# Two units' logits in one run of TensorE, on seven buffers for squares, in a fused Fourier, MLP and soft-MoE kernel

## The chip, the cores and the metric

One of the eight cores of a Trainium2 chip runs the whole program. The metric is the device time of one execution in microseconds. The kernel before took 2180.7 us as the median of three runs (2176.5 to 2181.17).

## What is computed

The reference runs three stages on `x` (8 sequences of 3072 tokens of 256 numbers):

```python
Y = irfft(soft_shrink(rfft(x, axis=1) @ (w_r + i w_i) + b))      # 24576 tokens x 256
h = np.maximum(Y @ w_in, 0.0);  z = (h * h) @ w_out              # MLP, 2048 hidden
logits = z @ phi                                                 # 32 slots
d = softmax(logits, over all tokens);  slot_in = d.T @ z         # 32 x 256
slot_out[e] = relu(slot_in[e] @ w1[e]) @ w2[e]                   # 8 experts, 4 slots each
out = softmax(logits, over slots) @ slot_out
```

The change lies in the second and third line of it: the MLP's hidden squares, their logits, and the sum over tokens that the dispatch softmax weighs. `phi` is multiplied into `w_out` ahead of time (`pw`), so logits come straight from the squares.

## The kernel before

A first part (about 530 us) does the Fourier transforms and leaves the tokens in DRAM. Then a loop does the MLP, the logits and the running dispatch sum; a tail of some 100 us does the experts and writes the output. The change is in the loop, and the order in which the loop's Python statements stand is the order of each engine's queue: the schedule is written out by hand, and an engine takes its instructions in that order.

The loop goes over 32 superblocks (`sb`) of 768 tokens, and in each over 8 units, so that n = 8 sb + r runs from 0 to 257, with r from 0 to 7. A `Unit` is 256 hidden columns for the superblock's tokens, in four quarters of 128 x 384 (`part(0)` to `part(3)`). Its work is spread over three iterations. In iteration n, `cur` is unit n, `p1` is unit n-1, `p2` is unit n-2:

- Products (TensorE, three matmuls each, `product`): `p0`, `p1`, `p5` of `cur`; `p4`, `p6`, `p2`, `p3` of the unit before. They go to the banks psA, psX (two of each, by parity of the unit) and psZ. `p0` and `p5` are each followed by a copy of psA to psX on ScalarE (L708, L716), onto which the next product of psX accumulates.
- The iteration's order on TensorE is p0, p4, p6, p1, p5, p2, p3, then `logits` of `p2` (tile `ls`). `add(3)` on VectorE (L735) reads psX after `p6`; `p3` accumulates onto the same psX and so waits for it. `add(1)` reads psA after `p2`.
- `relu` (ScalarE, L739) and `square` (L743) on GpSimd, but for `square(0)`, mostly on VectorE. `turn(1)` and `turn(0)` (VectorE, L747) transpose the squares into `gt` for the dispatch sum.
- `logits` multiplies the four quarters by `pw` with four matmuls on four 32-column strips, two records each.

Beside this, one superblock later, the routing of the block before (`s = sb - 1`) goes on at fixed r: `apart` at the end of r1 (ScalarE copies half of the logits, L807), `scores`, `lowest`, `exponents` and `weights` at r2 (maximum, exponentials, transposed through DRAM into `ee` by SP's queue, L828 and L830), the softmax over slots and `into_slots` at r3: 192 matmuls of 32 x 32 (`pz`, L765) into four banks. The iteration r4 has an order of its own (`else`): there `collect` (VectorE, L770) adds the four banks to `acc` while the next products start.

`stage_d` prepares the tokens of the superblock to come: at r0 and r1 two fills of 64 small matmuls (psY, L459), ScalarE's copies of them, and then some 20 casts and subtractions on GpSimd, of which `step(r, k)` lets k go at iteration r. `load_z` (SP) loads the tile `zt` for the one after that at the end of r5.

The squares lie in five buffers: three that the first halves take in turn, two for the second halves (`self.g`). The routing's scratch (`lw`, `lv`, `ew`, `et`, `co`) lies beside them in the same tile `wg`.

Of the kernel before, what the change touches and what calls it, by code (L numbers as in the profile page):

```python
# [29 lines left out]
TOK = TB * N1  # L30
# [73 lines left out]
def fft_moe_kernel(ctx, tc, x, w_r, w_i, b_r, b_i, moe_w_in, moe_w_out, moe2_phi, moe2_w1, moe2_w2,  # L104
# [384 lines left out]
    with tc.manual_schedule():  # L489
# [185 lines left out]
        def flat(o, n):  # L675
            return wgf[:, o:o + n]

        OG, OL, OZ, OE, OS = 0, 5 * GR, 5 * GR + TOK, 5 * GR + 3 * TOK, 6 * GR + 3 * TOK

        class Unit:  # L680


            def __init__(self, m):
                self.m = m
                self.s, i = divmod(m, NW)
                self.q = QS[self.s % 2][i]
                self.first, self.last = i == 0, i == NW - 1
                self.n = f"{self.s}_{self.q}"
                self.g = [flat(OG + GR * (m % 3), GR), flat(OG + GR * (3 + m % 2), GR)]

# [99 lines left out]

        lw, lv = flat(OL, HT), flat(OL + HT, HT)
        ew, et, co = (flat(OE + HT * i, HT) for i in range(3))
        ee = flat(OS, GR)
# [8 lines left out]

        def apart():

            for h in range(2):
                w, v = (slice(64 * i, 64 * i + 64) for i in (h, 1 - h))
                nc.scalar.copy(lv[w], lgp[v, HT * h:HT * h + HT])  # L807

        def scores():
            for h in range(2):  # L810
                w = slice(64 * h, 64 * h + 64)
                nc.vector.tensor_tensor(out=lw[w], in0=lgp[w, HT * h:HT * h + HT], in1=lv[w], op=ALU.add)

        def lowest(s):
            nc.vector.tensor_reduce(out=bx, in_=lw, axis=AX.X, op=ALU.max)
            nc.vector.scalar_tensor_tensor(out=nm[(s + 1) % 3], in0=bx, scalar=-1.0, in1=nm[s % 3], op0=ALU.mult, op1=ALU.min)

        def exponents(s):
            no, nn = nm[s % 3], nm[(s + 1) % 3]
            al[s], se[s] = (rt.tile([128, 1], F32, tag=t, name=f"{t}{s}", bufs=2) for t in ("al", "se"))  # L820
            nc.scalar.activation(out=ew, in_=lw, func=AF.Exp, bias=nn, accum_out=se[s])
            nc.scalar.activation(out=al[s], in_=no, func=AF.Exp, bias=nn, scale=-1.0)

        def weights(s):

            nc.vector.transpose(et, ew)
            d = dram.tile([32, GR], F32, tag="ed", name=f"ed{s}", bufs=2)
            nc.sync.dma_start(out=d.rearrange("p (c n) -> c p n", c=4), in_=et)  # L828
            for a in range(4):
                nc.sync.dma_start(wgf[32 * a:32 * a + 32, OS:OS + GR], d)  # L830

        def turn_rows():
            nc.vector.transpose(lts, lw)
            return lts.rearrange("p (k n) -> p k n", n=32)
# [54 lines left out]
        NM = NSB * NW  # L889
        run = side = None  # L890
        for n in range(NM + 2):
# [11 lines left out]
            def route(at):  # L903
                return s is not None and r == at

            if run is None:
                if cur:
                    cur.p0()
                step(1, 1)
                if p1:  # L910
                    p1.p4()
                step(1, 1)
                if route(2):
                    scores()
                    lowest(s)
                    exponents(s)
                step(2, 2)
                if p2 and r != 2:
                    p2.turn(1)
                if p1:  # L920
                    p1.p6()
                    p1.add(3, p1.x)
                if route(2):
                    weights(s)
                if p2 and r == 2:
                    p2.turn(1)
                if cur:
                    cur.p1()
                    cur.p5()
                if p2 and r not in (2, 3):  # L930
                    p2.turn(0)
                if p1:
                    p1.p2()
                    p1.add(1, p1.a)
                if p2 and r in (2, 3):
                    p2.turn(0)
                step(1, 1)
                if p1:
                    p1.relu(3)
                    p1.square(3, nc.gpsimd)  # L940
                    p1.p3()
                    p1.square(2, nc.vector if n == NM else nc.gpsimd)
                    p1.relu(1)
                    p1.square(1, nc.vector if n == NM else nc.gpsimd)
                if cur:
                    cur.square(0, nc.vector)
                if route(3):
                    cur.p4()
                    cur.p6()
                    drain(over_slots(turn_rows()))  # L950
                    keep(s, co)
                if p2:
                    p2.logits()
            else:
                sr, ps = run
                run = None
                p2.logits()
                p1.p3()
                p1.square(3, nc.gpsimd)
                p1.square(2, nc.gpsimd)  # L960
                collect(sr, 0, ps[0])
                collect(sr, 1, ps[1])
                cur.p0()
                p1.p2()
                p1.add(1, p1.a)
                collect(sr, 2, ps[2])
                p1.relu(1)
                p1.square(1, nc.gpsimd)
                collect(sr, 3, ps[3])
                cur.p1()  # L970
                cur.p5()
                cur.square(0, nc.gpsimd)
                p2.turn(1)
                p2.turn(0)
# [4 lines left out]
            if route(1):  # L979
                apart()  # L980
            if route(3):
                total(s)
            if r == 0 and sb + 1 < NSB:
                side = stage_d(sb + 1, bank, nc.gpsimd)
                next(side)
            step(2, 3)
            step(3, 10)
# [5 lines left out]
            if route(3):  # L993
                ps = [bank_a(n + 1, f"pz{s}_a"), bank_x(n + 1, f"pz{s}_x")] + [bank(f"pz{s}_{i}") for i in range(2)]
                into_slots(s, ps)
                cur.add(3, cur.x)
                cur.relu(3)
                run = (s, ps)
            if sb == NSB - 1 and r == 0:
                t = zp.tile([128, TB, DM], F32, tag="zt", name="ez").rearrange("p t d -> p (t d)")  # L1000
                for k in range(2):
                    load_w1(t[:, FE * k:FE * k + FE])
                load_wo()

# [7 lines left out]

        warm(1, "warm0")
        apart()
        for k in range(3):
            load_w1(wg[:, k])
        scores()
        lowest(s)
# [4 lines left out]
        for c in range(4):  # L1023
            w = slice(32 * c, 32 * c + 32)
            nc.tensor.matmul(pe[c], lhsT=same[w], rhs=ew[w], start=True, stop=True)
        p = bank("p_m")
# [15 lines left out]
        into_slots(s, ps)  # L1042
        lt = turn_rows()
        for k in range(3, 6):
# [176 lines left out]
```

## Time and profile before

| | before |
|---|---|
| median of three runs | 2180.7 us |
| profiled execution | 2177.24 us, span 2175.0 us |
| mean granted TensorE clock | 0.977 |
| TensorE busy | 2080.6 us (96%) |
| VectorE busy | 1543.0 us (71%) |
| ScalarE busy | 1277.2 us (59%) |
| GpSimd busy | 1317.5 us (61%) |
| matmuls of `ls` | 2048 records, busy 219.6 us |

The profile is of one execution. Busy time is the union of an engine's instructions; a matmul's record is longer than its share of the array, since products overlap (a record of 0.33 us, the next one 0.17 us later). So what an operation costs on TensorE is read from the starts of successive records. Where a row names a releaser, the engine sat idle for the time in brackets until that instruction ended.

### The profile page before, as it was taken

The page shows a single profiled execution, that of the slowest core. Times are in us where ns is not written, and L with a number is a line of the kernel's source. Part 1 is how long each engine was busy: PE and PEld are TensorE (multiplying, and loading weights), DVE is VectorE, ACT ScalarE, POOL GpSimd, SP SyncE. Part 2 cuts the span into 40 slices and gives each one's busy share as a digit, 9 for nine tenths or more (in the row PEclk, how much of TensorE's full clock was granted, in tenths as well). Part 3 has the DMA queues.
Part 4 walks back from the last instruction along what each step waited for, and adds up shares of the span by engine and source line. Part 5 has one row for each costly group of instructions (what it writes and reads, how often), then busy time and mean ns, then how long its engine had stood idle before and what let it go on. Part 6 is the DMA issues. An engine that isn't in the chain of part 4 may idle for free.

```text
span 2175.0 us, 55408 instructions
## 1 busy us (share of the span) xinstructions
PE 2080.6 (96%) x22294; PEld 1598.3 (73%) x22294; DVE 1543.0 (71%) x2590; ACT 1277.2 (59%) x2910; POOL 1317.5 (61%) x1583
## 2 busy tenths in 40 slices
PE   8999999998899999999999999999999999999994
PEld 3888888887777777777777777777777777777743
DVE  2677677766577777777777777777777777777743
ACT  2667666754565566566556665655666666556632
POOL 0243344411777777777777777777777777777500
PEclk7999999998999999999999999999999999999995
DMA  8988898863011111111111111111111111111589
GB/s 245 263 242 238 232 231 235 237 152 94 16 36 27 29 36 32 27 27 32 31 29 30 39 27 27 29 34 29 27 41 27 27 27 36 29 27 46 169 302 396
DMA packets 113772, 210.02 MB, mean 97 GB/s; under 512 B 14092, under 2 KB 80908, under 8 KB 107244
## 3 DMA queue, kind: packets, MB, share of 16 engines
q1 hardware_dynamic: 112348, 203.31, 34.6%
q8 instruction: 175, 2.87, 0.6%
q10 hardware_dynamic: 1168, 3.18, 0.4%
q14 instruction: 81, 0.66, 0.1%
HBM read 122.64 MB, written 83.79 MB: 95 GB/s over the span
## 4 chain that ended last, share of the span: by engine, by line
PE 69%; DVE 13%; DMA 5%; ACT 4%; POOL 4%; issue 4%; SPq 1%; DVEq 0%; ACTq 0%; POOLq 0%
PE psX L701 14%; PE psA L701 12%; PE ls L754 7%; DVE gt L747 4%; PE psZ L701 4%; PE pz_a L765 4%; PE psB L247 4%; PE psC L331 4%; PE psY L459 3%; PE pz_x L765 3%; POOL wg L743 3%; PE pz L765 3%; DVE wg L735 3%; PE psA L214 2%; ACT wg L739 2%
## 5 line engine op out<-in xcount | busy, mean ns | idle before, releaser
L743 POOL TENSOR_TENSOR wg<-wg 128x384 f32<-128x384 f32 x797 | 707.3, 910 | 371.3 <-ACT wg L739 368.9
L747 DVE STREAM_TRANSPOSE gt<-wg 128x768 f32<-128x768 f32 x512 | 487.9, 962 | 172.2 <-POOL wg L743 171.9
L739 ACT ACTIVATE wg<-psX 128x384 f32<-128x384 f32 x512 | 251.8, 492 | 269.4 <-PE psX L701 217.6
L701 PE MATMUL psX<-yh,wia 128*128 128x384 f32 x1024 | 364.9, 356 | 39.1 <-DVE wg L735 36.1
L701 PE MATMUL psA<-yh,wia 128*128 128x384 f32 x1024 | 362.2, 359 | 0.0
L739 ACT ACTIVATE wg<-wg 128x384 f32<-128x384 f32 x512 | 267.8, 523 | 139.7 <-DVE wg L735 139.6
L701 PEld LDWEIGHTS psA<-yh,wia 128*128 128x128 f32 x1024 | 192.3, 188 | 103.4 <-DVE wg L735 42.6
L701 PEld LDWEIGHTS psX<-yh,wia 128*128 128x128 f32 x1024 | 192.5, 188 | 95.8 <-DVE wg L735 56.6
L123 POOL TENSOR_TENSOR Sl<-Sf,Sh 128x256 fp32r<-128x256 f32 x96 | 75.4, 786 | 274.2 <-ACT Sh L122 239.8
L754 PE MATMUL ls<-wg 128*32 128x384 f32 x2048 | 219.6, 499 | 0.3 <-DVE wg L743 0.3
L765 PE MATMUL pz_x<-gt,wg 32*32 32x512 f32 x1584 | 209.2, 597 | 0.0
L765 PE MATMUL pz_a<-gt,wg 32*32 32x512 f32 x1584 | 208.9, 596 | 0.0
L765 PE MATMUL pz<-gt,wg 32*32 32x512 f32 x2976 | 203.5, 597 | 0.0
L743 DVE TENSOR_TENSOR wg<-wg 128x384 f32<-128x384 f32 x227 | 195.8, 863 | 7.8 <-ACT wg L739 7.7
L708 ACT COPY psX<-psA 128x384 f32<-128x384 f32 x256 | 119.6, 467 | 120.1 <-PE psA L701 119.7
L701 PE MATMUL psA<-yl,wia 128*128 128x384 f32 x512 | 172.4, 337 | 0.0
L701 PE MATMUL psZ<-yh,wib 128*128 128x384 f32 x512 | 172.1, 336 | 0.0
L701 PE MATMUL psX<-yl,wia 128*128 128x384 f32 x512 | 172.0, 336 | 0.0
L701 PE MATMUL psX<-yh,wib 128*128 128x384 f32 x512 | 171.6, 335 | 0.0
L701 PE MATMUL psA<-yh,wib 128*128 128x384 f32 x512 | 171.5, 335 | 0.0
L735 DVE TENSOR_TENSOR wg<-psX,wg 128x384 f32<-128x384 f32 x256 | 137.1, 536 | 42.5 <-ACT wg L722 32.0
L735 DVE TENSOR_TENSOR wg<-psA,wg 128x384 f32<-128x384 f32 x256 | 136.1, 532 | 41.0 <-PE psA L701 39.0
(211 smaller groups left out, 4807.5 us busy)
## 6 DMA issues: line engine op xcount, KB each, us to landing
bt<-ad SPq DMA_DIRECT2D x96, 256.0 KB
zd<-sc SPq DMA_DIRECT2D x96, 256.0 KB
zt<-zd SPq DMA_DIRECT2D x64, 384.0 KB
xt<-in_x_dram SPq DMA_DIRECT2D x126, 192.0 KB
ad<-sa SPq DMA_DIRECT2D x112, 192.0 KB
out_dram<-ob SPq DMA_DIRECT2D x21, 1024.0 KB
wg<-ed SPq DMA_DIRECT2D x124, 96.0 KB
w<-in_moe_w_dram SPq DMA_DIRECT2D x5, 1024.0 KB
```

The costliest lines, as they stand in the source:

```text
L123: (eng or nc.vector).tensor_tensor(out=lo, in0=v, in1=f(hi), op=ALU.subtract)
L247: nc.tensor.matmul(p[:, dh, :, l], lhsT=t[:, l, 128 * dh:128 * dh + 128], rhs=bm[:, 2 * (u % NU) + l], start=True, stop=True)
L331: nc.tensor.matmul(ps[l][:, v], lhsT=cm[w, (u - 1 + v) % NU, c], rhs=ub[v][w, c], start=c == 0, stop=c == 1)
L459: nc.tensor.matmul(ps[g][64 * c:64 * c + 64, tt::TB], lhsT=zt[s][w, tt, d:d + 64], rhs=dmt[w], start=True, stop=True)
L701: nc.tensor.matmul(p, lhsT=w[:, k, l], rhs=r[:, j], start=start and n == 0, stop=n == 2, skip_group_check=True)
L708: nc.scalar.copy(self.x, self.a)
L735: nc.vector.tensor_tensor(out=self.part(k), in0=p, in1=self.z, op=ALU.add)
L739: nc.scalar.activation(out=t, in_=t if p is None else p, func=AF.Relu)
L743: eng.tensor_tensor(out=t, in0=t, in1=t, op=ALU.mult)
L747: nc.vector.transpose(gt[:, 2 * self.q + a + window(self.s)], self.g[a])
L754: nc.tensor.matmul(lgp[o:o + 32], lhsT=pw[:, 2 * self.q + a], rhs=self.part(k), start=self.first, stop=self.last, skip_group_check=True)
L765: nc.tensor.matmul(ps[a][32 * c:32 * c + 32], lhsT=ee[w, c, k], rhs=gt[w, o:o + NT2, 32 * j:32 * j + 32], start=k == 0, stop=k == NB6 - 1, ...
```

## The change

- `logits` is no longer issued once in every iteration for unit n-2. It is issued in odd iterations, but for r3, for units n-3 and n-2 one behind the other, and at the head of the iteration r4 for the units of r0 and r1. So in a superblock there are four runs of two units: at the end of r1, at the head of r4, at the end of r5 and of r7.
- Since squares live longer, there are seven buffers for them, four and three. The routing's scratch moves out of `wg` into the unused end of the tile `zt` that `stage_d` works on (for the last block it stays in `wg`). The last superblock's two loads of expert weights into the `zt` tile move from r0 to r5.
- At r2, `relu(3)` moves ahead of `weights` and of the other relus, and the two steps of `stage_d` that stood in mid-iteration (ScalarE's copies of the second fill) move to the iteration's end.
- At r3, `add(3)` and `relu(3)` of the unit of r3 no longer stand behind `into_slots`; they stand in r4 behind collects 0 and 1. In r4, `p0` comes ahead of `p3`, and `collect` 3 moves to the end of r5.

```diff
-        OG, OL, OZ, OE, OS = 0, 5 * GR, 5 * GR + TOK, 5 * GR + 3 * TOK, 6 * GR + 3 * TOK
+        OZ, OS = 7 * GR, 7 * GR + TOK
...
-                self.g = [flat(OG + GR * (m % 3), GR), flat(OG + GR * (3 + m % 2), GR)]
+                self.g = [flat(GR * (m % 4), GR), flat(GR * (4 + m % 3), GR)]
...
-        lw, lv = flat(OL, HT), flat(OL + HT, HT)
-        ew, et, co = (flat(OE + HT * i, HT) for i in range(3))
+        def scratch(s):
+
+            if s == NSB - 1:
+                z, o = wgf, 4 * GR
+            else:
+                z, o = zt[min(s + 2, NSB - 1)].rearrange("p t d -> p (t d)"), 2 * TOK
+            return [z[:, o + HT * i:o + HT * i + HT] for i in range(5)]
+
...
                 if route(2):
-                    scores()
+                    scores(s)
                     lowest(s)
                     exponents(s)
-                step(2, 2)
                 if p2 and r != 2:
                     p2.turn(1)
                 if p1:
                     p1.p6()
                     p1.add(3, p1.x)
+                if p1 and r == 2:
+                    p1.relu(3)
                 if route(2):
                     weights(s)
...
                 if p1:
-                    p1.relu(3)
+                    if r != 2:
+                        p1.relu(3)
                     p1.square(3, nc.gpsimd)
...
                 if route(3):
                     cur.p4()
                     cur.p6()
-                    drain(over_slots(turn_rows()))
-                    keep(s, co)
-                if p2:
+                    drain(over_slots(turn_rows(s)))
+                    keep(s, scratch(s)[4])
+                if n % 2 and p2 and not route(3):
+                    units[n - 3].logits()
                     p2.logits()
             else:
-                sr, ps = run
+                sr, ps = late = run
                 run = None
-                p2.logits()
+                units[n - 4].logits()
+                units[n - 3].logits()
+                collect(sr, 0, ps[0])
+                collect(sr, 1, ps[1])
+                p1.add(3, p1.x)
+                p1.relu(3)
+                cur.p0()
                 p1.p3()
                 p1.square(3, nc.gpsimd)
                 p1.square(2, nc.gpsimd)
-                collect(sr, 0, ps[0])
-                collect(sr, 1, ps[1])
-                cur.p0()
                 p1.p2()
+                collect(sr, 2, ps[2])
                 p1.add(1, p1.a)
-                collect(sr, 2, ps[2])
                 p1.relu(1)
                 p1.square(1, nc.gpsimd)
-                collect(sr, 3, ps[3])
                 cur.p1()
                 cur.p5()
...
-            step(2, 3)
+            if late and r == 5:
+                collect(late[0], 3, late[1][3])
+            step(2, 5)
             step(3, 10)
...
                 into_slots(s, ps)
-                cur.add(3, cur.x)
-                cur.relu(3)
                 run = (s, ps)
-            if sb == NSB - 1 and r == 0:
+            if sb == NSB - 1 and r == 5:
                 t = zp.tile([128, TB, DM], F32, tag="zt", name="ez").rearrange("p t d -> p (t d)")
                 for k in range(2):
                     load_w1(t[:, FE * k:FE * k + FE])
+            if sb == NSB - 1 and r == 0:
                 load_wo()
```

## Rows read from the trace of the kernel before

**Rows 1.** Busy us of each engine in a stretch, then clock, DMA share, GB/s
```profile
core 0: us, PE busy (x) PEld busy (x) DVE busy (x) ACT busy (x) POOL busy (x), PEclk, DMA share, GB/s
1000.00:1200.00 200.00, 195.39 (x2262) 148.77 (x2260) 152.80 (x240) 120.60 (x278) 153.48 (x183) 1.00 0.16 33
```

**Rows 2.** TensorE's waits over the span: total us, times, longest us
```profile
PE psX L701 <- DVE wg L735: 36.1, 63, 6.0
```

**Rows 3.** Timeline of TensorE, r6: start us, duration us; first, third of p0
```profile
1004.36 0.44 PE L701 MATMUL psA<-yh,wia 128*128 128x384 f32 x1
...
1004.82 0.34 PE L701 MATMUL psA<-yh,wia 128*128 128x384 f32 x1
...
1007.94 0.34 PE L701 MATMUL psX<-yh,wia 128*128 128x384 f32 x1
1008.21 0.85 PE L754 MATMUL ls<-wg 128*32 128x384 f32 x8
1008.99 0.45 PE L701 MATMUL psA<-yh,wia 128*128 128x384 f32 x1
1009.27 0.34 PE L701 MATMUL psA<-yl,wia 128*128 128x384 f32 x1
```

**Rows 4.** Timeline of TensorE, 1008.8 to 1008.9: the second four of that visit
```profile
1008.55 0.51 PE L754 MATMUL ls<-wg 128*32 128x384 f32 x4
```

**Rows 5.** Timeline of TensorE around the second psY fill, r1
```profile
1022.43 0.34 PE L701 MATMUL psA<-yh,wia 128*128 128x384 f32 x1
1022.70 1.15 PE L459 MATMUL psY<-dmt,zt 48*64 48x48 f32 x64
1023.78 0.45 PE L701 MATMUL psX<-yh,wia 128*128 128x384 f32 x1
```

**Rows 6.** Timeline of TensorE, r3: p1's first two, p2's last, p3's first
```profile
1031.64 0.44 PE L701 MATMUL psX<-yh,wia 128*128 128x384 f32 x1
1031.92 0.34 PE L701 MATMUL psX<-yl,wia 128*128 128x384 f32 x1
...
1033.14 0.34 PE L701 MATMUL psA<-yh,wia 128*128 128x384 f32 x1
1033.92 0.44 PE L701 MATMUL psX<-yh,wia 128*128 128x384 f32 x1 [0.44 <-DVE wg L735]
```

**Rows 7.** Timeline of TensorE, r4: p2's last and p1's first product
```profile
1045.27 0.34 PE L701 MATMUL psA<-yh,wia 128*128 128x384 f32 x1
1045.68 0.44 PE L701 MATMUL psX<-yh,wia 128*128 128x384 f32 x1
```

**Rows 8.** Timeline of TensorE, r5: p2's last and p3's first product
```profile
1049.78 0.34 PE L701 MATMUL psA<-yh,wia 128*128 128x384 f32 x1
1050.62 0.44 PE L701 MATMUL psX<-yh,wia 128*128 128x384 f32 x1 [0.51 <-DVE wg L735]
```

**Rows 9.** Timeline of ScalarE, r2 and r3: the fill's copies, r3's copy to psX
```profile
1028.25 0.83 ACT L476 COPY zt<-psY 128x384 f32<-128x384 f32 x2
...
1031.10 0.49 ACT L708 COPY psX<-psA 128x384 f32<-128x384 f32 x1
```

**Rows 10.** Timelines of VectorE and GpSimd, r6 to r7
```profile
1008.26 0.55 DVE L743 TENSOR_TENSOR wg<-wg 128x384 f32<-128x384 f32 x1
1008.31 1.19 POOL L743 TENSOR_TENSOR wg<-wg 128x384 f32<-128x384 f32 x1 [0.61 <-ACT wg L739]
...
1011.22 0.52 DVE L735 TENSOR_TENSOR wg<-psX,wg 128x384 f32<-128x384 f32 x1
```

**Rows 11.** Timelines of VectorE and GpSimd, r4: collects 2 and 3, four squares
```profile
1046.12 1.40 DVE L770 SCALAR_TENSOR_TENSOR acc<-acc,al,pz 128x512 f32<-128x512 f32 x2
1047.04 3.18 POOL L743 TENSOR_TENSOR wg<-wg 128x384 f32<-128x384 f32 x4
```

**Rows 12.** Timeline of SP's queue, r3: the exponents' four copies
```profile
1031.48 1.70 SPq L830 DMA_DIRECT2D wg<-ed  x4
```

**Rows 13.** Timeline of TensorE: the first of pz
```profile
1036.48 0.61 PE L765 MATMUL pz_a<-gt,wg 32*32 32x512 f32 x1
```

**Rows 14.** The page's second section: GB/s in 40 slices of the span
```profile
GB/s 245 263 242 238 232 231 235 237 152 94 16 36 27 29 36 32 27 27 32 31 29 30 39 27 27 29 34 29 27 41 27 27 27 36 29 27 46 169 302 396
```

More of the change, by code (lines that the diff above doesn't have):

```diff
@@ L801, in keep, with apart @@
                 nc.sync.dma_start(out=cd[64 * h:64 * h + 64, r, HT * c:HT * c + HT], in_=co[64 * c:64 * c + 64])
-        def apart():
+        def apart(s):
+            lv = scratch(s)[1]
             for h in range(2):
@@ L807, in apart, with scores @@
                 nc.scalar.copy(lv[w], lgp[v, HT * h:HT * h + HT])
-        def scores():
+        def scores(s):
+            lw, lv = scratch(s)[:2]
             for h in range(2):
@@ L814, in lowest @@
         def lowest(s):
+            lw = scratch(s)[0]
             nc.vector.tensor_reduce(out=bx, in_=lw, axis=AX.X, op=ALU.max)
@@ L818, in exponents @@
         def exponents(s):
+            lw, _, ew = scratch(s)[:3]
             no, nn = nm[s % 3], nm[(s + 1) % 3]
@@ L824, in weights @@
         def weights(s):
+            ew, et = scratch(s)[2:4]
             nc.vector.transpose(et, ew)
@@ L830, in weights, with turn_rows @@
                 nc.sync.dma_start(wgf[32 * a:32 * a + 32, OS:OS + GR], d)
-        def turn_rows():
-            nc.vector.transpose(lts, lw)
+        def turn_rows(s):
+            nc.vector.transpose(lts, scratch(s)[0])
             return lts.rearrange("p (k n) -> p k n", n=32)
@@ L889, in fft_moe_kernel @@
         NM = NSB * NW
-        run = side = None
+        run = side = late = None
         for n in range(NM + 2):
@@ L979, in fft_moe_kernel @@
             if route(1):
-                apart()
+                apart(s)
             if route(3):
@@ L1013, in fft_moe_kernel @@
         warm(1, "warm0")
-        apart()
+        apart(s)
         for k in range(3):
             load_w1(wg[:, k])
-        scores()
+        scores(s)
         lowest(s)
@@ L1024, in fft_moe_kernel @@
             w = slice(32 * c, 32 * c + 32)
-            nc.tensor.matmul(pe[c], lhsT=same[w], rhs=ew[w], start=True, stop=True)
+            nc.tensor.matmul(pe[c], lhsT=same[w], rhs=scratch(s)[2][w], start=True, stop=True)
         p = bank("p_m")
@@ L1042, in fft_moe_kernel @@
         into_slots(s, ps)
-        lt = turn_rows()
+        lt = turn_rows(s)
         for k in range(3, 6):
```

## The prediction, made before the changed kernel was timed

> **What bounds the kernel now.** Read first the busy time by stretch, for a stretch in the middle of the token loop: TensorE is busy 195.4 of 200 us at a granted clock of 1.00, the full level of 2.4 GHz, while VectorE and GpSimd stand near 153 and ScalarE at 121 [rows 1]. So the loop, about 1500 of the 2175 us, goes at TensorE's pace, and an edit is worth what it takes from TensorE's issue times. Read next what TensorE waited for: 36.1 us in 63 pieces, all named as the sums that VectorE makes from psX (L735) [rows 2]; two pieces in each of the 31 superblocks that carry an earlier block's routing. Busy time hides a second loss, which shows only in start times. Read therefore the timeline of TensorE alone, and look at distances from start to start.
>
> **One visit to the logits.** From the third product of p0 to the third of p3 lie 18 products in 3.12 us, 0.173 us each [rows 3]. The step into `ls` is 0.27 us, so entry costs 0.10. The eight `ls` records last 0.78 to the next psA. The step from that psA to the next product is 0.28, so leaving costs 0.11 [rows 3]. Inside, the second four records start 0.34 after the first four, but psA starts 0.44 after the second four [rows 3, 4]: the last group also pays 0.10 to empty the array. A lone visit thus costs 0.10 + 0.78 + 0.11 = 0.99 us for two steps of 0.34.
>
> **What the change does to visits.** Write r0 to r7 for a superblock's eight iterations. Before, TensorE leaves its 128x128 products eight times: r0 (ls, then psY), r1 twice (psY; ls), r2, r3 with r4 (ls, pz, ls), r5, r6, r7. After, six times: r0 (psY alone), r1 twice (psY; two ls), r3 with r4 (pz, two ls), r5, r7 (two ls each). The psY fill that stands alone enters at the same price (0.27 from psA to psY) and lasts 1.08 [rows 5]; I take that for r0 too.
> - Two visits less: 2 x (0.10 + 0.11) = 0.42 us.
> - Four pairs: 3 x 0.34 + 0.44 = 1.46 instead of 2 x 0.78 = 1.56; four times 0.10 = 0.40. No row shows four groups in one run; the bounds are 1.46 (the step inside stays 0.34) and 1.56 (each unit keeps its price). I take 1.46, since the step inside is a row of the same instruction.
> Together 0.82 us a superblock, with 0.42 as the lower bound.
>
> **The waits of before**, as steps over 0.173. A product after a pause makes the next one late by 0.11 (0.28 from first to second) [rows 6]. In r3: 0.11 at p1, then 0.78 - 0.17 + 0.11 = 0.72 at p3 [rows 6]. In r4: 0.41 - 0.17 + 0.11 = 0.35 at p1 [rows 7]. In r5: 0.84 - 0.17 + 0.11 = 0.78 at p3 [rows 8]. Sum 1.96 us.
>
> **The waits of after**, iteration by iteration; nothing of this is in the trace, each is worked out from when its inputs came before.
> - r2 to r3. The logits visit at r2's end (0.99) is gone, so TensorE comes to r3's p1 that much sooner. p1 needs ScalarE's copy L708, which ended at 1031.10 + 0.49 and held p1 already [rows 6, 9]. The two psY copies (0.83 us) [rows 9] move from the middle of r2 to its end, still ahead of L708, and relu(3) goes forward: the same operations in another order, so L708 doesn't move. That gives 0.99 + 0.11 = 1.10 at most. It is less if the routing, which starts behind r1's logits, moves back by less than the 0.68 that a pair is longer; 0.42 if not at all. I estimate 0.85, as ScalarE still has r1's own relus ahead of that. It takes over from the one at r3's p3: VectorE's turn there waits for GpSimd's squares, and those start sooner with relu(3) ahead of the two copies (0.83 less in front of it). So p3's 0.72 goes, and 0.85 at p1 comes.
> - r3 and r4. `add(3)` no longer hides under pz; it queues behind collects 0 and 1, which need pz's end. Collect takes 0.70 [rows 11], add 0.52 [rows 10]: 0.70 + 0.70 + 0.52 + 0.05 = 1.97 us after pz. p3 waits for it, and behind p3 stand p2, p1 and the whole rest. The cover is the two logits (1.46) and p0 (0.11 + 3 x 0.173): 2.09. So nothing, with 0.1 to spare; without p0 ahead of p3 it would be 0.5. The copy that p1 waited for now has p3 and p2 before it: r4's 0.35 goes.
> - r5. Collect 3 (0.70) leaves the queue ahead of r5's add(3), but the add of r4 (0.52) has come into it; and GpSimd's four squares of r4, 3.18 us in a row [rows 11], keep their place behind ten side operations, starting some 0.7 sooner. The turn at r5 needs the first two squares. TensorE comes to p3 later by one unit's logits, 0.68, and sooner by the waits that went. I get a wait of 0.2 + 0.11 = 0.3 (0 to 0.8) for the 0.78 of before.
> - r7, new. The chain that lets p3 go runs from r6: relu(3), two GpSimd squares, VectorE's turn, add(3), and it is tied to r6's p5 and not to the logits. It ended at 1011.22 + 0.52, 7.38 after r6's p0 at 1004.36 [rows 3, 10]. Without logits at r6, r7's p0 comes 21 x 0.173 + 0.11 = 3.75 after r6's, and p3 18 x 0.173 later, at 6.87. It waits 0.56 with a signal of 0.05, and 0.11 after it: 0.67. At r1 the same chain is covered by two fills of over 1 us each.
> - The exponents for pz. Their transposed copies are issued from 1031.48 to 1033.18, 3.3 us ahead of pz at 1036.48 [rows 12, 13]; that shrinks to about 1.8. No row shows the landing. The cost lies between nothing and 0.5; I take nothing, as nothing waits there now.
> After: 0.85 + 0.3 + 0.67 = 1.82 against 1.96.
>
> GpSimd's first square of r6 took 1.19 us where four in a row took 0.80 each, and VectorE's own square started 0.05 before it and lasted 0.55 [rows 10, 11]. The Trainium skill (SBUF — State Buffer, "Who interferes with whom") says that a VectorE instruction with two SBUF inputs contends with a GpSimd one that reads SBUF, and that the second to issue is blocked until the first is done. By that rule the square would have taken 0.50 + 0.80 = 1.30; the row is 0.11 below, and with the rule's number r7's wait would be 0.78 and the forecast 3.4 us later.
>
> **The rest.** Seven buffers for five add no instruction: a unit's first half is written again four units on and its second three on, when its logits are already issued. The routing's scratch in `zt` makes SP's next load of `zt` wait also for the stores of `co`; that load already waits for GpSimd's work on the tile and is wanted three iterations later. In the last superblock two loads of 512 KB go from r0 to r5; if the tail waited for them, 1 MB at the 302 GB/s of the slice before the last [rows 14] is 3.5 us at most; I take nothing, since later loads of the same size still follow. In superblock 0 the longest wait, 6.0 us [rows 2], hides logits that are now behind it; what the pairs gain there and what is uncovered are about equal. At the end the last two logits are issued in the same place.
>
> **Sum.** 0.82 + (1.96 - 1.82) = 0.96 us a superblock, 31 of them: 30 us. The profiled execution took 2177.2 us (span 2175.0 and 2.2 around it), 3.5 below the median of 2180.7 and inside the runs. 2177.2 - 30 = 2147.
>
> **Rivals.**
> - More waits go. If the copies at r2's end don't hold p1 and r5 waits for nothing, only r7's 0.67 stays: 0.82 + 1.29 = 2.11, 65 us, 2112. For it: GpSimd and VectorE have a quarter of their time free [rows 1]. Against: L708 held p1 already [rows 6]. Chance 0.18.
> - The pair keeps twice its price: 0.42 + 0.14 = 0.56, 17 us, 2160. Against: the 0.34 inside a run. Chance 0.05.
> - The gain is eaten. If r5's wait stays at 0.78 and add(3) at r4 is late by 0.4, saved and lost are equal: 2177. Chance 0.08.
> - Slower: VectorE's queue between pz's end and r5's add(3) bounds. If it is not shorter than before, r3, r4 and r5 lose their 1.96 as now, and r3's 0.85 at p1 and r7's 0.67 come on top: 0.82 - 1.52 = -0.70, or 22 us more, 2199. It decides once the new waits exceed 0.82 with the old in place. For it: the new add stands in that queue. Against: a collect left it, and the second logits give 0.68 more cover. Chance 0.09.
>
> **How the numbers follow.** The forecast has 0.60; the likeliest time is 2147. Its own bounds: pairs 0.42 to 0.82, waits of after 1.3 to 2.6, give 2177 - 46 = 2131 to about 2177. The range goes from 2108, to take in the first rival, to 2172, which leaves out the last two. Faster by over 0.2%, about what a measurement of this kernel can tell from no change: 0.60 + 0.18 + 0.05 = 0.83; same 0.08; slower 0.09.
>
> **What would show it.** Right: `ls` comes in runs of sixteen, 1.46 us to the next product; six departures a superblock; a wait at r3's p1 for L708 and at r7's p3 for add(3), none at r4's p3; a superblock near 46.8 us. Wrong: sixteen `ls` in 1.56 or more, a wait of psX for add(3) at r4, pz waiting for a DMA, or a wait in r1.

## The result, and the profile after

| | before | after |
|---|---|---|
| median | 2180.51 us (2176.5 to 2181.17, 4 runs) | 2156.75 us (2152.05 to 2161.37, 4 runs) |
| ratio, 95% interval | | 0.9895 [0.9868, 0.9921] |
| profiled execution (span) | 2177.24 (2175.0) | 2152.05 (2150.3) |
| a superblock, mean of 28 (least, most) | 47.77 us (47.75, 47.82) | 46.99 us (46.74, 48.06) |

The change gains 1.05%: 24 us of the 30 forecast. The time lies 10 us above the forecast and inside the range; about half of the 10 is that the forecast was made against the profiled execution, whose counterpart after took 2152.05. The last line is the better measure for what follows: the distance from one superblock's first psY fill to the next one's, mean over those whose records are whole. It leaves out the Fourier part: the loop's first product started between 531.4 and 538.3 us in the profiled executions of all the runs. 0.785 us times 31 superblocks are 24.3 us, so the whole gain lies in the loop, and every experiment below is read by this length, which comes from one profiled execution of each kernel. Where the text gives means of steps on TensorE, they are distances from start to start over the same superblocks, with 0.173 us a product taken off.

The busy time by stretch, kernel after, same columns as [rows 1]: TensorE is busy 197.1 of 200 us instead of 195.4, with 2336 records for 2262, in part because the stretch begins at another place of a superblock.

```profile
1000.00:1200.00 200.00, 197.06 (x2336) 155.09 (x2335) 151.50 (x240) 121.16 (x281) 154.13 (x182) 1.00 0.14 29
```

TensorE's waits over the span, after (total us, times, longest). The 63 pieces on psX of [rows 2] are gone but for two; 33 pieces on psA have come, about one a superblock. It is the same line L735, yet another sum: `add(1)`, which reads psA, not `add(3)`. A wait for a DMA shows too, once. Shorter holds lie within the length of the records and show in the start times alone.

```profile
PE psA L701 <- DVE wg L735: 18.4, 33, 0.6
PE psX L701 <- DVE wg L735: 6.4, 2, 6.2
PE pz_a L765 <- DMA wg<-ed: 0.5, 1, 0.5
```

**The pair.** Timeline of TensorE around the logits at the end of r7 (start us, duration us). Sixteen records in one run, 1.42 from the first to the next psA, where two visits took 2 x 0.78 [rows 3]; the mean over all pairs is 1.427. The products of p3 in front of it stand at 1003.41 to 1004.21: 0.34 from the last of p2 to the first of p3 shows a wait at p3 of 0.34 - 0.17, and 0.28 to the second the late start that follows one.

```profile
1003.41 0.34 PE L701 MATMUL psA<-yh,wia 128*128 128x384 f32 x1
1003.75 0.45 PE L701 MATMUL psX<-yh,wia 128*128 128x384 f32 x1
1004.03 0.34 PE L701 MATMUL psX<-yl,wia 128*128 128x384 f32 x1
...
1004.47 1.50 PE L754 MATMUL ls<-wg 128*32 128x384 f32 x16
1005.89 0.44 PE L701 MATMUL psA<-yh,wia 128*128 128x384 f32 x1
```

**r3 after.** TensorE, then VectorE, then ScalarE; this answers [rows 6, 9]. r2's last product starts at 1020.96, r3's p0 only at 1021.88: VectorE's `turn(1)`, then `add(1)` of r2 hold it. `add(1)` ends at 1021.82 and reads the psA bank that p0 writes. Then p1 comes at 1023.58, 0.18 behind the last of p6 and 0.05 after ScalarE's copy L708 (to 1023.53), which stands behind the two psY copies. L708 thus holds p1 by no more than 0.02, and the late start behind it is most of p1's cost.

```profile
1020.96 0.34 PE L701 MATMUL psX<-yh,wia 128*128 128x384 f32 x1
1021.88 0.44 PE L701 MATMUL psA<-yh,wia 128*128 128x384 f32 x1 [0.58 <-DVE wg L735]
...
1023.40 0.34 PE L701 MATMUL psX<-yh,wib 128*128 128x384 f32 x1
1023.58 0.45 PE L701 MATMUL psX<-yh,wia 128*128 128x384 f32 x1
...
1020.44 0.94 DVE L747 STREAM_TRANSPOSE gt<-wg 128x768 f32<-128x768 f32 x1
1021.30 0.52 DVE L735 TENSOR_TENSOR wg<-psA,wg 128x384 f32<-128x384 f32 x1
...
1022.28 0.86 ACT L476 COPY zt<-psY 128x384 f32<-128x384 f32 x2
1023.01 0.52 ACT L708 COPY psX<-psA 128x384 f32<-128x384 f32 x1
```

**r7 after.** r6's last product at 999.89, r7's p0 at 1000.36: again `add(1)` of the iteration before, to 1000.30. No logits stand between them any more.

```profile
999.89 0.34 PE L701 MATMUL psX<-yh,wia 128*128 128x384 f32 x1
1000.36 0.44 PE L701 MATMUL psA<-yh,wia 128*128 128x384 f32 x1
...
999.74 0.56 DVE L735 TENSOR_TENSOR wg<-psA,wg 128x384 f32<-128x384 f32 x1
```

**r4 after.** TensorE, then VectorE. `add(3)` waits behind two collects and ends at 1035.69; p3 starts at 1035.82. The two logits and p0 cover it, but for some 0.05.

```profile
1033.76 1.50 PE L754 MATMUL ls<-wg 128*32 128x384 f32 x16
1035.19 0.44 PE L701 MATMUL psA<-yh,wia 128*128 128x384 f32 x1
1035.82 0.37 PE L701 MATMUL psX<-yh,wia 128*128 128x384 f32 x1
...
1034.48 0.74 DVE L770 SCALAR_TENSOR_TENSOR acc<-acc,al,pz_x 128x512 f32<-128x512 f32 x1
1035.14 0.55 DVE L735 TENSOR_TENSOR wg<-psX,wg 128x384 f32<-128x384 f32 x1
```

**r5 after.** TensorE's last product of p4 and first of p6, 0.33 apart, and ScalarE: copy L716, for which p6 waits, ends at 1039.10, because two relus stand ahead of it and the first of them waited for a sum.

```profile
1038.82 0.34 PE L701 MATMUL psZ<-yh,wib 128*128 128x384 f32 x1
1039.15 0.44 PE L701 MATMUL psX<-yh,wib 128*128 128x384 f32 x1
...
1037.70 0.53 ACT L739 ACTIVATE wg<-wg 128x384 f32<-128x384 f32 x1 [0.58 <-DVE wg L735]
1038.13 0.47 ACT L739 ACTIVATE wg<-psX 128x384 f32<-128x384 f32 x1
1038.64 0.46 ACT L716 COPY psX<-psA 128x384 f32<-128x384 f32 x1
```

**pz after.** SP's queue and the first pz; this answers [rows 12, 13]. The last of the four copies is issued by 1025.49, 1.44 ahead of pz. That is one of the two shortest leads; on the mean of the superblocks it is 1.78, where 3.19 (3.3 in the rows) lay between them before. pz lasts 6.72 on the mean (6.51 to 7.56) instead of a steady 6.51. The packets in the trace show when the copies land. Before, the last packet landed 1.83 ahead of pz's start on the mean, and never less than 0.74; after, 0.35 on the mean, from 0.62 ahead to 0.48 behind it. In the 18 superblocks of 29 in which pz took over 6.55, it ended 6.94 to 7.16 behind that landing; in the 11 others the landing lay 0.40 ahead or more. So what lengthens pz is the landing.

```profile
1023.80 1.69 SPq L839 DMA_DIRECT2D wg<-ed  x4
...
1026.93 0.61 PE L765 MATMUL pz_a<-gt,wg 32*32 32x512 f32 x1
```

A microsecond of that transfer by the busy time (columns of [rows 1]): the DMA engines still move 197 GB/s at a share of 0.69.

```profile
1025.00:1026.00 1.00, 1.00 (x8) 1.00 (x7) 0.52 (x2) 0.90 (x2) 0.92 (x2) 1.00 0.69 197
```

The whole account of a superblock, in us:

| | before | forecast after | after |
|---|---|---|---|
| time in the logits | 6.26 | 5.84 | 5.71 |
| entries and exits saved | | 0.42 | 0.52 |
| waits r3 | 0.83 | 0.85 | 1.01 |
| waits r4 | 0.35 | 0 | 0.05 |
| waits r5 | 0.78 | 0.30 | 0.29 |
| waits r7 | 0 | 0.67 | 0.67 |
| pz, longer or later | 0 | 0 | 0.23 |
| gain | | 0.96 | 0.785 |

Saved is 0.55 in the logits and 0.52 at entries and exits; the waits, with pz's, grow from 1.96 to 2.25. (The forecast took a lone visit at 0.78, so 6.24 before and a saving of 0.40 in the logits.)

### The profile page after: what moved, and what is told of

It is laid out like the page before. It is cut to its first block, busy times and chain, and to the rows that moved or that the text cites. A ratio compares the mean times of both kernels' runs of the same rounds, so it can differ in the third digit from the quotient of the medians.

```text
span 2150.3 us, 55350 instructions
## 1 busy us (share of the span) xinstructions
PE 2059.2 (96%) x22294; PEld 1621.0 (75%) x22294; DVE 1542.0 (72%) x2590; ACT 1268.5 (59%) x2910; POOL 1312.2 (61%) x1583
## 4 chain that ended last, share of the span: by engine, by line
PE 82%; DVE 7%; DMA 4%; ACT 3%; issue 1%; POOL 1%; SPq 1%; DVEq 0%; POOLq 0%; ACTq 0%
PE psA L701 18%; PE psX L701 16%; PE ls L754 8%; PE psZ L701 5%; PE psB L247 4%; PE psC L331 4%; PE pz L765 4%; PE pz_a L765 4%; PE psY L459 3%; PE pz_x L765 3%; PE psA L214 2%; PE psL L117 2%; PE psL L118 2%; PE psL L119 2%; DVE wg L735 2%; DMA out_dram<-ob 2%
## 5 line engine op out<-in xcount | busy, mean ns | idle before, releaser
L701 PE MATMUL psA<-yh,wia 128*128 128x384 f32 x1024 | 369.1, 360 | 22.6 <-DVE wg L735 18.4
L701 PE MATMUL psX<-yh,wia 128*128 128x384 f32 x1024 | 356.6, 348 | 7.0 <-DVE wg L735 6.4
L765 PE MATMUL pz_x<-gt,wg 32*32 32x512 f32 x1584 | 215.2, 597 | 0.2 <-issue 0.2
L765 PE MATMUL pz_a<-gt,wg 32*32 32x512 f32 x1584 | 214.9, 597 | 0.5 <-DMA wg<-ed 0.5
L754 PE MATMUL ls<-wg 128*32 128x384 f32 x2048 | 193.6, 495 | 0.3 <-DVE wg L743 0.3
L708 ACT COPY psX<-psA 128x384 f32<-128x384 f32 x256 | 120.7, 472 | 121.0 <-PE psA L701 117.7
L743 DVE TENSOR_TENSOR wg<-wg 128x384 f32<-128x384 f32 x227 | 181.2, 799 | 7.1 <-ACT wg L739 7.0
L735 DVE TENSOR_TENSOR wg<-psA,wg 128x384 f32<-128x384 f32 x256 | 138.0, 539 | 54.5 <-PE psA L701 50.7
L735 DVE TENSOR_TENSOR wg<-psX,wg 128x384 f32<-128x384 f32 x256 | 138.6, 541 | 38.3 <-PE psX L701 29.5
```

The source lines that it names most:

```text
L701: nc.tensor.matmul(p, lhsT=w[:, k, l], rhs=r[:, j], start=start and n == 0, stop=n == 2, skip_group_check=True)
L708: nc.scalar.copy(self.x, self.a)
L735: nc.vector.tensor_tensor(out=self.part(k), in0=p, in1=self.z, op=ALU.add)
L743: eng.tensor_tensor(out=t, in0=t, in1=t, op=ALU.mult)
L754: nc.tensor.matmul(lgp[o:o + 32], lhsT=pw[:, 2 * self.q + a], rhs=self.part(k), start=self.first, stop=self.last, skip_group_check=True)
L765: nc.tensor.matmul(ps[a][32 * c:32 * c + 32], lhsT=ee[w, c, k], rhs=gt[w, o:o + NT2, 32 * j:32 * j + 32], start=k == 0, stop=k == NB6 - 1, ...
```

## Experiments

Each was timed beside runs of the kernel before on the same chip (medians 2181 to 2183 us). After's ratio to compare with is 0.9895, its superblock 46.99.

### Which wait holds r3: e1, e2, e3

Theory A: r3's holds (p0 by `add(1)`, p1 by L708, p3 by `add(3)`) stand in series on chains that end at nearly the same time, so a move that frees one gives little. Its rival B: the hold at p0 is a cost of its own, and comes back when `add(1)` comes earlier. The prediction had L708 alone.

e1: `turn(1)` of r2 behind `add(1)`.

```diff
-                if p2 and r == 2:
-                    p2.turn(1)
...
                     p1.add(1, p1.a)
+                if p2 and r == 2:
+                    p2.turn(1)
```

> The changed kernel with one move at r2: the turn of the unit before goes behind add(1) on VectorE, so add(1), which r3's p0 waits for, comes about 0.5 us sooner. Theory A (two holds in series at r3: p0 behind add(1), and p1 behind ScalarE's copy L708, which ended 0.05 us before p1): p0's pause falls from 0.74 to about 0.26, p1's grows from 0.13 to about 0.6, the superblock stays within 0.1 us of 46.99 and the time near 2155. Theory B (add(1) alone holds r3): the superblock shortens by 0.5 to 0.6 and the time by 15 to 19 us, to about 2139.

Measured: 2163.34 us, ratio 0.9911 [0.988, 0.9942], superblock 47.19. p0's hold fell from 0.74 to 0.29; p1's rose from 0.02 to 0.48, and p3, free before, came 0.21 late, each with a late start of 0.11 behind it. TensorE's waits over the span have a new line, of 31 pieces:

```profile
PE psX L701 <- ACT psX L708: 10.1, 31, 0.6
```

And its timeline in r3, the last product of p6 and the first of p1:

```profile
1029.45 0.34 PE L701 MATMUL psX<-yh,wib 128*128 128x384 f32 x1
1030.12 0.44 PE L701 MATMUL psX<-yh,wia 128*128 128x384 f32 x1 [0.33 <-ACT psX L708]
```

The hold moved to the next link, as A says; B falls. But A allowed 0.1 a superblock, and it became 0.2 longer: r3's waits are 1.3 in all, not 1.01. The hold at p3 is the move's own doing at least in part: with the turn behind `add(1)`, r3's `add(3)` starts 4.10 us behind `add(1)` by VectorE's timeline, where it was 2.82.

e2: the fill's two copies ahead of the routing's first copy at r1's end, instead of at r2's end.

```diff
+            step(1, 2)
...
-            step(2, 5)
+            step(2, 3)
```

> The changed kernel with ScalarE's two copies of the second fill moved from r2's end to r1's end, where ScalarE sat idle 0.56 us before the logits. It takes some 0.73 us out of the queue ahead of L708 at r3. The prediction's theory (L708 holds r3, 0.85 us): about 0.85 a superblock less, 26 us, near 2130. Theory A or B (p0 is held by add(1)): only p1's 0.13 goes, 4 us, near 2152.

Measured: 2164.81 us, 0.9912 [0.9878, 0.9946], superblock 47.21. Neither theory had a loss. p1's hold is gone, but p0's grew to 0.95 and pz to 6.88; as p0 now comes later by more than p1's hold was, this run alone doesn't show that the copies held L708. The copies (0.85 us) now stand ahead of the routing's first copy (L813), where ScalarE had 0.56 us of idle time in e1; the routing starts later (its first store is issued 0.20 later, counted from the second psY fill), and with it the VectorE operations ahead of `add(1)`. ScalarE's timeline of e2:

```profile
1026.74 0.85 ACT L476 COPY zt<-psY 128x384 f32<-128x384 f32 x2
1027.61 0.64 ACT L813 COPY zt<-ls 64x192 f32<-64x192 f32 x2
```

Its waits of TensorE: the pieces behind `add(1)` grew from 18.4 to 25.1 us.

```profile
PE psA L701 <- DVE wg L735: 25.1, 34, 0.8
```

e3: both edits.

> Both moves at once. Theory A: r3's pauses fall from 1.0 to about 0.4 in sum, more than the two moves alone give together. What becomes of it is open: if the exponents' transfer is what pz waits for (pz lasts 6.72 on average against 6.51 before the change), pz gets longer by what is gained, some 0.5, and the time stays within 5 us of 2155 to 2150; if pz's extra 0.2 has another cause, 0.6 a superblock or 19 us is gained, near 2137.

Measured: 2166.59 us, 0.9926 [0.9902, 0.995], superblock 47.20. p0 0.29, p1 0.04, p3 0.23: r3 in all 0.81, 0.2 less than in the kernel after. With `add(1)` early in both, the copies are the one difference to e1, and p1's hold falls from 0.48 to that 0.04: L708 did hold it by way of those copies. Of the 31 pieces of e1 two are left:

```profile
PE psX L701 <- ACT psX L708: 1.2, 2, 0.6
```

But pz rose to 7.11 (6.83 to 8.28), and the time lies above what A allowed. The third link is the exponents' way through DRAM: what r3 no longer waits, pz does, ending 7.04 behind the landing on the mean (6.89 to 7.14). The landing itself comes 0.19 later than in the kernel after, since the copies ahead of the routing start it 0.20 later; pz's end comes 0.17 later with it, most of the 0.21 by which e3's superblock is longer.

### Is it the transfer? e5, e6, e9

To shorten the exponents' way, the four copies of 96 KB became one of 384 KB whose source repeats (e6 on the kernel after; e5 the same with e3's moves).

```diff
-            for a in range(4):
-                nc.sync.dma_start(wgf[32 * a:32 * a + 32, OS:OS + GR], d)
+            nc.sync.dma_start(wgf[:, OS:OS + GR], d.unsqueeze(0).broadcast_to([4, 32, GR]))
```

> Both moves at r2 and r1 as in the earlier run of both, and the four copies of the exponents (SP, 0.4 us of issue each) made one copy to all 128 partitions, which takes 1.2 us of issue out of the way to pz. Theory A (three holds in series: add(1), L708, the exponents' transfer): pz falls from 7.11 to 6.51, the superblock from 47.20 to about 46.5 and the time by some 18 to 22 us, near 2145. Rival C (pz got longer for another reason than the transfer, as TensorE's own order): pz stays near 7.1 and the time near 2165.

> The changed kernel with the one copy of the exponents alone, in place of the four. Theory A: pz falls from 6.72 on average to 6.51, r3's holds stay (0.74 and 0.13), so 0.2 a superblock, 6 us, near 2150, and the spread of the superblocks (46.7 to 48.0) goes. Rival C: no difference.

Measured: e5 2348.96 us, 1.0766 [1.0747, 1.0784], superblock 53.11; e6 2349.2 us, 1.077 [1.0754, 1.0786], 53.07. Both expectations missed, by some 200 us. e6's waits of TensorE now name the copies:

```profile
PE pz_a L765 <- DMA wg<-ed: 85.1, 20, 6.5
```

Its timeline, SP's queue and then TensorE's last product ahead of pz and the first pz:

```profile
1034.46 0.57 SPq L838 DMA_DIRECT2D wg<-ed  x1
...
1037.66 0.34 PE L701 MATMUL psX<-yh,wib 128*128 128x384 f32 x1
1041.56 1.03 PE L765 MATMUL pz_a<-gt,wg 32*32 32x512 f32 x1 [3.56 <-DMA wg<-ed]
```

Its busy time by stretch (columns of [rows 1]):

```profile
1037.00:1039.00 2.00, 1.00 (x6) 0.67 (x4) 2.00 (x4) 1.27 (x3) 2.00 (x3) 1.00 0.25 78
1039.00:1041.00 2.00, 0.00 (x0) 0.00 (x0) 1.50 (x4) 0.36 (x1) 1.92 (x4) 0.93 0.17 63
1041.00:1043.00 2.00, 1.44 (x32) 0.49 (x33) 1.86 (x6) 0.00 (x0) 1.92 (x3) 0.50 0.00 0
```

The one copy spares SP 1.1 us of issuing and still lands about 5.1 us after its first packet (1035.84 to 1040.95), where the four took 2.0 (1024.74 to 1026.74): the DMA share stays at 0.25 or below, 78 GB/s, against 0.69 and 197 GB/s. The Trainium skill (DMA: Bandwidth & Descriptors, "Rules for kernel authors") says that a leading zero-stride repetition of c copies confines a DMA to at most c of the 16 engines; four of sixteen is the 0.25 of the row. The trace agrees, and read beforehand the rule would have spared the miss. Then pz itself takes 8.55 us on the mean instead of 6.72: behind the wait of 3.56 us its first part goes at a granted clock of 0.50, the lower level of 1.2 GHz. e6 was meant as a gain; it serves as the dose instead. On the mean of the superblocks the landing comes 3.8 us later and pz starts 4.2 later. Eleven more pieces of that wait, 47.4 us, are put down to VectorE's softmax over slots, but whichever is named, pz starts 0.6 to 1.1 behind the last packet in every superblock. So pz does hang on this transfer.

e9: e3's two moves, and two of the four copies issued by ScalarE's queue at r3, so that SP issues only two.

```diff
-            for a in range(4):
+            for a in range(2):
...
+                if route(3):
+                    for a in range(2, 4):
+                        nc.scalar.dma_start(wgf[32 * a:32 * a + 32, OS:OS + GR], eds[s])
```

> Both moves (add(1) ahead of the turn at r2, the fill's copies at r1), and of the exponents' four copies two are issued by SP as before and two by ScalarE's queue at r3, so that the last is issued some 0.6 us sooner. Theory A (the transfer is the third hold): pz falls from 7.11 by 0.4 to 0.6, the superblock from 47.20 to 46.6 to 46.8, the time by 12 to 18 us to some 2150. Rival: what ScalarE spends on issuing (0.4 to 0.6 us each) holds r3's relu and copies, and r3's pauses grow by as much: no gain, near 2165.

Measured: 2163.34 us, 0.9918 [0.9897, 0.9939], superblock 47.19; pz 6.93 for e3's 7.11. The last copy was issued 0.9 us sooner, the data landed 0.35 us sooner (5.7 for 6.05 us after the first issue of the chain, from the packets): most of what SP's queue took was not on the path. The expected 46.6 to 46.8 was not reached, and the time is near the rival's 2165: what pz gained came back at r3's p6 (0.06, where three pieces now name ScalarE's copy L716) and at r5's p3 (0.08).

### What is the pairing itself worth? e4

e4: everything of the change but the pairs: one unit's logits in each iteration.

```diff
-                if n % 2 and p2 and not route(3):
-                    units[n - 3].logits()
+                if p2:
                     p2.logits()
...
-                units[n - 4].logits()
-                units[n - 3].logits()
+                p2.logits()
```

> The changed kernel with logits of one unit in every iteration again, as before, and all the rest of the change kept. Theory P (visits cost, but a lone visit also covers other holds): eight visits cost 1.09 us a superblock more; the pauses at r3 (1.0), r7 (0.67) and in pz (0.2) go since logits stand in front of them, a new one of about 0.65 comes at r4's p3; in sum within 0.4 of 46.99, time 2145 to 2165. Theory Q (the pairs are the whole gain of the change): back to 47.8 or more, time 2175 to 2190.

Measured: 2156.9 us, 0.9873 [0.9844, 0.9903], superblock 46.98, the same as with the pairs (46.99). The eight lone visits take 6.34 us instead of 5.71, and two departures come back; but r3's waits shrink to 0.1, r7's to nothing, and pz's to 0.07, since a visit again lies between p3 and the next p0. New is a hold of 0.61 in r4: one visit ends too soon to cover collects 0 and 1 and `add(3)`. TensorE and VectorE in r4:

```profile
1041.52 0.85 PE L754 MATMUL ls<-wg 128*32 128x384 f32 x8
...
1042.84 0.33 PE L701 MATMUL psA<-yh,wia 128*128 128x384 f32 x1
1043.51 0.44 PE L701 MATMUL psX<-yh,wia 128*128 128x384 f32 x1 [0.34 <-DVE wg L735]
...
1042.25 0.74 DVE L770 SCALAR_TENSOR_TENSOR acc<-acc,al,pz_x 128x512 f32<-128x512 f32 x1
1042.90 0.55 DVE L735 TENSOR_TENSOR wg<-psX,wg 128x384 f32<-128x384 f32 x1
```

So what the pairs save at the array, the cover that they take away costs again, and the other edits (relu(3), the two sums, the copies) carry the whole gain that is measured. The pairs without the other edits were not run, so what they would bring alone is not shown.

### Taking the new waits away: e7, e8, e10, e11, e12

e7: `relu(3)` early at r6 as at r2. e8: `relu(1)` and `square(1)` of r4 behind p5 of r4.

```diff
-                if p1 and r == 2:
+                if p1 and r in (2, 6):
...
-                    if r != 2:
+                    if r not in (2, 6):
```

```diff
                 p1.add(1, p1.a)
-                p1.relu(1)
-                p1.square(1, nc.gpsimd)
                 cur.p1()
                 cur.p5()
+                p1.relu(1)
+                p1.square(1, nc.gpsimd)
```

> The changed kernel with relu(3) moved forward at r6 as it is at r2, ahead of ScalarE's copy that waits for p5. The prediction's chain for r7 (relu(3), two squares, turn, add(3), p3) starts about 0.5 us sooner: p3's pause at r7 (0.14 and 0.11 after it) goes. The other half of r7's wait stays, p0 behind r6's add(1) (0.30 and 0.11): 0.25 a superblock, 8 us, near 2149. If the chain were the only hold, all 0.67 would go: 21 us, near 2136.

> The changed kernel with relu(1) of r4 moved behind ScalarE's work for p1 and p5. Theory: r5's pause is p6 waiting for the copy L716, which stands behind relu(1), which waits for add(1); with the move the pause (0.16 and 0.13) goes: 0.29 a superblock, 9 us, near 2148. The prediction's theory for r5 (the turn and add(3) behind GpSimd's squares) gives no difference, since those squares don't move forward.

e7: 2150.2 us, 0.9859 [0.9844, 0.9873], superblock 46.76. r7's hold at p3 (0.25) is gone, that at p0 (0.41) stays: both as expected, so the first hangs on `relu(3)` and the second does not. e8: 2154.03 us, 0.9874 [0.986, 0.9889], superblock 46.88. The hold at r5's p6 (0.16) is gone with its late start (0.11). But p1, not held before, comes 0.03 late behind the next copy on ScalarE, L708 (to 1040.97), with a late start of 0.11 and some 0.04 behind it: 0.11 of the 0.29 is gained. TensorE and ScalarE in e8:

```profile
1041.02 0.45 PE L701 MATMUL psX<-yh,wia 128*128 128x384 f32 x1
...
1040.49 0.48 ACT L708 COPY psX<-psA 128x384 f32<-128x384 f32 x1
```

e10: e7; `p2` and `add(1)` ahead of p5 at r6; `relu(1)` and `square(1)` of r4 behind r5's p0.

```diff
+                if late and r == 5:
+                    p2.relu(1)
+                    p2.square(1, nc.gpsimd)
...
+                swap = cur and p1 and r in (6,)
...
+                if swap:
+                    p1.p2()
+                    p1.add(1, p1.a)
```

> The changed kernel with three moves away from r3: relu(3) of r6 forward; p2 and add(1) of r6 ahead of p5, so that add(1) is done when r7's p0 comes; relu(1) and square(1) of r4 behind r5's p0. Theory from the holds read in the trace: r7's 0.67 goes whole, r5's 0.29 nearly: 0.9 a superblock, 28 us, near 2128. Rival (p5's copy, now 0.52 later, holds r7's p6, or the turn takes add(1)'s place): r7 keeps 0.3 or more and the time stays above 2138.

Measured: 2147.52 us, 0.9842 [0.9825, 0.9859], superblock 46.69. r7's 0.67 became 0.23, r5's 0.29 became 0.12; but 0.29 came at r6's p0, which neither theory had, so the 2128 was not reached. TensorE and VectorE there: the turn waits 1.10 us for GpSimd's square that now comes late, `add(1)` stands behind it until 1044.67, and p0 starts 1.59 behind the first logits, not 1.43 (1.72 on the mean).

```profile
1043.13 1.50 PE L754 MATMUL ls<-wg 128*32 128x384 f32 x16
1044.72 0.44 PE L701 MATMUL psA<-yh,wia 128*128 128x384 f32 x1
...
1043.25 0.98 DVE L747 STREAM_TRANSPOSE gt<-wg 128x768 f32<-128x768 f32 x1 [1.10 <-POOL wg L743]
1044.15 0.52 DVE L735 TENSOR_TENSOR wg<-psA,wg 128x384 f32<-128x384 f32 x1
```

e11: all of these moves (the swap of p2 at r2 too) with e3's and e9's.

> All moves together: those of r6 and r4, p2 and add(1) ahead of p5 at r2 as well, the fill's copies at r1, the exponents' copies on two queues. If the holds add up as read: r3's 0.9, r7's 0.67, r5's 0.25 go, pz stays within 0.2 of 6.51: superblock 45.2, time near 2100. If the exponents' transfer bounds the stretch from r2's maximum to pz: r3's gain comes back in pz, superblock 46.0, time near 2126, no better than without the moves at r2 and r1.

Measured: 2161.45 us, 0.9903 [0.9883, 0.9922], superblock 46.96. Both expected lengths, 45.2 and 46.0, were missed. r3's hold at p0 falls to 0.09; 0.25 at p1, 0.17 and a late start at p3, 0.34 in r5, 0.35 at r6's p0, and pz at 6.95 eat it.

e12: e10, with the logits at r2 given back as cover: one unit at r2's end, two at r4's head, one at r5's end.

```diff
+                if r == 2 and s is not None:
+                    p2.logits()
+                elif r == 5 and s is not None:
+                    p2.logits()
-                if n % 2 and p2 and not route(3):
+                elif n % 2 and p2 and not route(3):
...
-                units[n - 4].logits()
                 units[n - 3].logits()
+                p2.logits()
```

> The moves of r6 and r4 (the run before with those alone: superblock 46.69, 2147.5 us), and one lone visit put back where the holds are: the logits of r0's unit at r2's end, those of r1 and r2 at r4's head, r3's alone at r5; r1 and r7 keep their pairs. Theory (logits at r2's end cover add(1), L708 and the exponents' transfer at once): a visit more costs 0.3, r3's pauses fall from 1.0 to 0.3 or less, pz from 6.75 to 6.51: superblock 45.8 to 46.1, time 2120 to 2130. Rival (the holds only move on to r4 and r5, as the ones at r3 did in the runs before): within 0.2 of 46.69, time 2142 to 2153.

Measured: 2146.93 us, 0.9842 [0.9829, 0.9856], superblock 46.67: as the rival had it. r3 has no hold left (the visit at r2's end covers 1.0 us for 0.37), and pz stands at 6.68. But the lone visit at r5 no longer covers what delays r6: its own second half and then p0, behind `add(1)`, come 0.96 late in all. TensorE:

```profile
1041.40 1.12 PE L754 MATMUL ls<-wg 128*32 128x384 f32 x8
1043.14 0.44 PE L701 MATMUL psA<-yh,wia 128*128 128x384 f32 x1 [0.61 <-DVE wg L735]
```

e10 and e12 are the fastest kernels of the study, some 10 us below the change as given. A lone visit at r2's end without the edit of r4, which should not bring on r6's hold, was not tried.

## Why the prediction was right, point by point

- **The direction and the mechanism.** The loop goes at TensorE's issue times, and 31 times the change of a superblock is the whole gain: right (24.3 us; 23.8 between the medians). `ls` comes in runs of sixteen and TensorE leaves its products six times, as forecast. But the superblock is 46.99 and not near 46.8. And the books hold for the change as a whole, not for the pairs: e4, without them, has the same superblock, since the other edits then take as much out of the waits. The prediction did not ask what the pairs alone are worth.
- **Two visits less, 0.42.** Measured 0.52: behind a lone visit p0 and p4 lose 0.14 together, not the 0.11 that the first step shows, and behind a pair only 0.11.
- **Four pairs, 0.40.** Undersized: 0.55. A pair took 1.427, 0.03 below the 1.46 put together from single steps; 0.34 a group of four was the right end of the bounds, and the rival that a pair keeps twice its price falls.
- **r2 to r3, 0.85 at p1.** The size was near (1.01) by luck, the holder wrong. The prediction followed psX alone (L708, then `add(3)`) and left out the psA bank that r2's `add(1)` frees for r3's p0. The visit at r2's end had covered that too. e1, e2 and e3 show three links one behind the other, L708 the second of them.
- **r4, none.** Right: 0.05, with the cover of two logits and p0; e4, with one, pays 0.61.
- **r5, 0.3.** Right in size (0.29) by luck, wrong in place: it stands at p6, behind ScalarE's copy L716 (0.16, and 0.11 of late start), not at p3 behind the turn. e8 takes it away there, and 0.18 come back right behind it, most of it at p1 after the copy L708.
- **r7, 0.67.** Right in sum. But 0.41 of it is p0 behind r6's `add(1)`, again the bank left out; TensorE comes that much later to p3, whose wait shrinks to 0.25. The end of the chain was right, so the sum was; e7 takes away the p3 part alone.
- **pz, nothing.** Wrong: 0.23, inside the bounds of 0 and 0.5. The lead from the last issue was right (1.78 on the mean for 1.8), but the term took a lead of issue for enough: the last packet lands 1.43 behind that issue on the mean (1.18 to 2.56), and pz's length follows the landing, as e6 shows too. The packets in the trace before show the landing, 1.83 ahead of pz; that was to be set against the loss of 1.5. The text had named a wait of pz for a DMA as a sign against it; that sign came.
- **GpSimd's square.** The first square of r6 took 1.19 us again, and r7 came out at the 0.67 that the row gave. The prediction's other estimate, 0.78, was made from the rule of the Trainium skill (SBUF — State Buffer, "Who interferes with whom") that of a VectorE instruction with two SBUF inputs and a GpSimd one that reads SBUF the second is blocked until the first is done. With two holds in it, the sum is no sharp test of the rule.
- **The rivals.** More waits gone (2112) would have needed r3 and r5 free; the gain eaten (2177) and the slower queue (2199) an `add(3)` late at r4, which the two logits hide.
- **The bounds.** They were added up too narrowly: 0.42 saved with waits of 2.6 makes 2184, not about 2177, and the 2.6 (1.10, 0.8 and 0.67) leaves out the 0.5 that pz could cost. The measured time lies far inside either way.

In sum the pairs and departures gave 0.25 more a superblock than put down, and the waits took 0.43 more (0.16 at r3, 0.05 at r4, 0.23 at pz): 0.18 less than 0.96, or 5.6 us over 31 superblocks. Two errors of opposite sign made the forecast look closer than its terms were.

## What to carry to other kernels

A matmul run that is taken out of a place was also the cover of everything that frees the banks of the next products: go through every operand and every output bank of the first few products behind it, not only the wait that the trace names, since that is merely the last of several links. Where links stand in series, a move that frees one of them gives little; so follow the chain to its end rather than to its first hold. Count a transfer's lead from its landing, which the packets show, and not from its issue. Price the grouping of work on a bound engine against a version with every edit but the grouping (here e4): the saving at the array and the lost cover came out equal.

## What the runs showed of the hardware that was not expected

- One DMA of 384 KB with a repeated source landed in 5.1 us where four of 96 KB, issued one after another, took 2.0; the DMA share never passed 0.25 in it, and the kernel lost 190 us against the kernel after.
- The exponents' way through DRAM, from the first issue to the last landing, took 6.05 us on the mean in the kernel after, but 5.77 to 7.15 from one superblock to another, and pz's spread of 6.51 to 7.56 follows it.
- In e6 TensorE's granted clock went from 1.00 to 0.50 near the end of the wait of 3.56 us, and pz took 8.55 us on the mean instead of 6.72.
- Two units' logits in one run cost 1.427 us, 0.71 a unit against 0.78 alone, and the products behind a run of sixteen recover sooner (0.63 and 0.52 for the first two parts) than behind one of eight (0.645 and 0.53).
